# Keys of two batches turned by VectorE through DRAM instead of by TensorE

## The chip, the cores and the metric

One of the cores of a Trainium2 chip runs the kernel. The metric is the device time of one execution in microseconds: before the change the median of 3 runs is 856.25 us (856.16 to 856.46).

## The reference, cut to what matters

Linear attention over 4 batches, 8 heads, 576 positions and 64 numbers per head; its output goes through two feed-forward layers (512 to 2048 to 512), the first with ELU, the second with Mish. All in float32.

```python
q_s = softmax(q, axis=-1)                      # over the 64 numbers of a head
k_s = softmax(k, axis=2)                       # over the 576 positions
kv  = einsum('bhsd,bhse->bhde', k_s, v)        # 64 x 64 per head
x   = einsum('bhsd,bhde->bhse', q_s, kv)       # heads side by side: 2304 x 512
h   = x @ w_in;  g = where(h > 0, h, exp(min(h, 0)) - 1);  x = g @ w_out
h   = x @ w2_in; g = h * tanh(log1p(exp(min(h, 20))));     out = g @ w2_out
```

## The kernel before

**Numbers.** The weights come as 64-bit numbers, 512 KB for a piece of 128 rows. A piece is loaded raw, its exponent is moved by ScalarE (`rebias`), it is put together by VectorE (`decode`), and it is split into a high and a low part (`split_piece`: ScalarE the high one, GpSimd the low one). Activations are split the same way, and each product is three matmuls: low times high, high times low, high times high.

**Blocks and slots.** The 18 tiles of 128 tokens form five blocks of 4, 3, 4, 3 and 4 tiles (`TILES`), so 512 or 384 columns. Layer 1 goes block by block; a block has 16 slots, one for each piece of 128 hidden numbers. In slot f TensorE makes h of piece f (12 matmuls, `mm_h`), then whatever else the slot holds, and then adds piece f-2 to the output y (12 matmuls, `mm_y`). y has four PSUM banks, and the last slot of a block is followed by `end_y`, which splits them into the input of layer 2; that is emitted at the end of slot 1 of the next block, and each bank is free for the new block when ScalarE has copied its high part and VectorE has subtracted it. Two DMAs on GpSimd's queue then store the two parts to DRAM, 1 MB each for block 0. Layer 2 starts after block 4.

**What lies beside it.** While block j runs, the attention of the next tiles is made, and raw pieces of layer 2's weights are loaded, split and stored to DRAM. The function `at(j, f, where, ...)` puts a step into a slot, and `where` is its place there: "pre", "load", "mid", "pe", "post", "last", "late", in this order for every engine's queue; nothing is reordered later. The steps of head pair hp of a batch (two heads, 128 rows of the transposed key, 576 positions in five chunks of 128, the last with 64) count from slot s = 2 hp - 1 in blocks 1 and 2 (where batches 2 and 3 are made):

- `load_k` in s-2 and `load_v` in s+2, both by SyncE. There are three key buffers (`kT`) and one value buffer (`v`).
- `k_max` (VectorE) and `k_exp` (ScalarE) in s, with the positions along the free dimension.
- `k_turn` and `k_turn_rest` in s+1: TensorE transposes four chunks of 128 and one of 64 into PSUM; `k_turned` and `k_turned_rest`: ScalarE copies them back into the same tile.
- `k_kv` in s+3: the product of the turned key with the value, 20 passes in the trace. It stands ahead of the transposes of the next head pair in the same slot.
- `k_scale`: ScalarE scales it into the block-diagonal tile that `q_x` uses.

Query tiles already go another way in blocks 1 to 3: `q_out` stores the tile to DRAM, `q_in` fetches it back by four DMAs, one for each group of 32 partitions, so that 32 x 32 blocks change places, and `q_blocks` lets VectorE transpose every 32 x 32 block in place. `q_x` then multiplies the tile with the block-diagonal tile. SyncE issues all of these DMAs in the order of the program, and an issue that waits holds all behind it.

The constants by name: `P` is 128, `DM` is 512, `NC` is 5 (chunks of positions), `NHP` is 4 (head pairs). `L263` and so on in the rows are lines of the program before: 263 `k_turn`, 280 `k_turn_rest`, 297 `k_kv`, 428 `mm_h`, 477 `mm_y`, 487 `end_y`, 241 `k_max`, 359 and 364 `q_sum` and `q_norm`, 332 `q_blocks`, 154 `decode_low`, 161 `decode_join`, 443 `elu_join`, 461 `split_lo`, 218 `load_k`, 225 and 229 `load_v`, 319 `q_out`, 326 `q_in`, 133 a raw piece.

Of the kernel before, what the change touches and what calls it, by code (L numbers as in the profile page):

```python
# [8 lines left out]
F32 = mybir.dt.float32  # L9
F32R = mybir.dt.float32r  # L10
U32 = mybir.dt.uint32
# [5 lines left out]
P = 128  # L17
# [23 lines left out]
def attention_elu_mish(  # L41
# [15 lines left out]
    nc = tc.nc  # L57
    B, DM, S = kT.shape
# [3 lines left out]
    NHP = DM // P  # L62
# [6 lines left out]
    TILES = (4, 3, 4, 3, 4)  # L69
    NA = len(TILES)  # L70
    assert sum(TILES) * P == NT
    at0 = [sum(TILES[:j]) for j in range(NA)]
# [42 lines left out]

    raw = {}
    w_hi, w_lo, split_t = {}, {}, {}
    w_src = {("i", 0): w1_in, ("o", 0): w1_out, ("i", 1): w2_in, ("o", 1): w2_out}  # L120

    def load_piece(kind, layer, f, t=None):
        w = w_src[kind, layer]
        if t is None:
            t = stage.tile([P, 512, 2], U32, tag="raw", name="raw", bufs=4)
        c = slice(f * P, (f + 1) * P)
        if kind == "i":
            nc.sync.dma_start(
                out=t.rearrange("p (k c) two -> p k (c two)", c=P),
                in_=w[:, c, :].rearrange("(k p) c two -> p k (c two)", p=P),  # L130
            )
        else:
            nc.sync.dma_start(out=t, in_=w[c, :, :])
        raw[kind, layer, f] = t
# [75 lines left out]
    def load_k(b, hp, t=None):  # L210
        if t is None:
            t = ap.tile([P, NC, P], F32, tag="kT", name="kT", bufs=3)
        en_t[b, hp] = t

        if S % P:
            nc.gpsimd.memset(t[S % P:P, S // P, S % P:P], 0.0)
        t = t.rearrange("p c e -> p (c e)")[:, 0:S]
        nc.sync.dma_start(out=t, in_=kT[b, hp * P:(hp + 1) * P, :])
        k_t[b, hp] = t
# [13 lines left out]
    def load_q(i, t=None):  # L233
        if t is None:
            t = ap.tile([P, DM], F32, tag="q", name="q")
        nc.sync.dma_start(out=t, in_=q[i * P:(i + 1) * P, :])
        q_t[i] = t
# [13 lines left out]
    def inverse(s):  # L251
        nc.vector.tensor_scalar(out=s, in0=s, scalar1=EPS, scalar2=None, op0=ALU.add)
        nc.vector.reciprocal(out=s, in_=s)
# [60 lines left out]

    R = 32

    def q_out(i):
        d = dram.tile([P, DM], F32, name=f"turn_q{i}")
        nc.sync.dma_start(out=d, in_=q_t[i])
        turn_t[i] = d  # L320

    def q_in(i):

        d = turn_t.pop(i).rearrange("(a j) (h r i) -> r j h a i", j=R, r=P // R, i=R)
        for r in range(P // R):
            nc.sync.dma_start(
                out=q_t[i][r * R:(r + 1) * R, :].rearrange("j (h a i) -> j h a i", h=NHP, i=R),
                in_=d[r],
            )

    def q_blocks(i):
        nc.vector.transpose(out=q_t[i], in_=q_t[i])

    NH = DM // D

# [1 line left out]
        return q_t[i].rearrange("p (h d) -> p h d", d=D)  # L337

    def load_q3(i):
        t = ap.tile([P, NC, P], F32, tag="kT", name="kT", bufs=3)  # L340
        load_q(i, t.rearrange("p c e -> p (c e)")[:, 0:DM])

    def q_max(i):
        m = sp.tile([P, NH], F32, tag="qm", name="qm")
# [272 lines left out]
    def at(j, f, where, fn, *a):  # L617
        j, f = j + f // NF, f % NF
        beside.setdefault((j, f, where), []).append((fn, a))
# [5 lines left out]
    def kv_chain(j, f, b):  # L625
        for hp in range(NHP):

            s = f + 2 * hp
            if j or hp > 2:
                at(j, s - 2, "load", load_k, b, hp)  # L630
            if (b, hp) not in v_t:
                at(j, s + 2, "load", load_v, b, hp)
            at(j, s, "late", k_max, b, hp)
            at(j, s, "late", k_exp, b, hp)
            at(j, s + 2, "post", lambda b, hp: inverse(rk_t[b, hp]), b, hp)
            at(j, s + 3, "post", k_scale, b, hp)


            rest = s + 1 if j else s + 2
            if j and hp:  # L640
                at(j, s + 1, "pe", k_kv, b, hp - 1)
            at(j, rest, "pe", k_turn_rest, b, hp)
            at(j, rest, "pe", k_turned_rest, b, hp)
            if not j or hp == NHP - 1:
                at(j, s + 3, "pe", k_kv, b, hp)
            at(j, s + 1, "pe", k_turn, b, hp)
            at(j, s + 1, "pe", k_turned, b, hp)

    def q_chain(j, f, i, o):
        at(j, f - 2, "late", load_q3 if j and o == 2 else load_q, i)  # L650
        at(j, f - 1, "late", q_max, i)
        at(j, f - 1, "late", q_less, i, NORM[j])
        at(j, f, "mid", q_exp, i)
        at(j, f, "late", q_sum, i)
        at(j, f, "late", q_norm, i, NORM[j])
        for fn in (q_x, x_hi, x_lo):
            at(j, f + (5 if j else 2), "pe", fn, i)
        if j:
            at(j, f + 1, "late", q_out, i)
            at(j, f + 2, "late", q_in, i)  # L660
            at(j, f + 4, "post", q_blocks, i)
            return
        for fn in (q_turn, q_turned):
            at(j, f + 1, "pe", fn, i)
# [11 lines left out]
    for j in range(NA - 1):  # L676
        if j + 1 < B:
            kv_chain(j, -1 if j else 0, j + 1)
        for o in range(TILES[j + 1]):
            q_chain(j, 9 - 3 * (TILES[j + 1] - 1 - o) if j else 8 + 2 * o, at0[j + 1] + o, o)  # L680

    for n in range(NF):
        j, s = 1 + n // 4, n % 4 * 4
# [241 lines left out]
```

## Time and profile before

| what | us |
|---|---|
| median of 3 runs | 856.25 |
| the profiled execution | 856.38 |
| its span, first to last instruction | 854.6 |
| TensorE busy | 843.7 (99% of the span) |
| VectorE busy | 599.4 (70%) |
| ScalarE busy | 451.1 (53%) |
| GpSimd busy | 160.3 (19%) |

The granted clock of TensorE is 0.999 of full speed over the span. An engine's busy time counts its own instructions, not the issue of DMAs; a matmul's duration overlaps with the next, so what a matmul costs is read from the distance between two starts. Block 1 runs from about 121.9 to 199.9 us and block 2 from there to about 286 us.

### The profile page before, as it was taken

How to read it: one execution, taken by the hardware profiler on the slowest of the kernel's cores; microseconds unless marked ns; L12 is line 12 of the kernel's file. 1: busy time of each engine (PE TensorE's matmuls, PEld its weight loads, DVE VectorE, ACT ScalarE, POOL GpSimd, SP SyncE). 2: the span in 40 equal slices, each digit the busy share in tenths (PEclk: the TensorE clock that was granted, in tenths of full speed). 3: DMA queues.
4: the chain of work that ended last, by engine and by line, in shares of the span. 5: the costliest groups of instructions: out<-in, count | busy, mean ns of one | idle time of the engine just before them, and what ended most of it. 6: DMA issues, size and time to landing. Idle time of an engine off the chain costs nothing.

```text
span 854.6 us, 11819 instructions
## 1 busy us (share of the span) xinstructions
PE 843.7 (99%) x4364; PEld 728.6 (85%) x4364; DVE 599.4 (70%) x1051; ACT 451.1 (53%) x854; POOL 160.3 (19%) x210
## 2 busy tenths in 40 slices
PE   7999999999999999999999999999999999999998
PEld 5778889998888899988889998888888888888996
DVE  7899866665555577554446877777787777777776
ACT  7797757656554465554444444444444444444443
POOL 4366523233212242223332000000000000000000
PEclk9999999999999999999999999999999999999999
DMA  9791648673845196538876003000210021000101
GB/s 302 251 306 55 197 129 279 182 231 98 232 131 161 52 265 196 166 99 286 278 243 227 1 0 103 34 1 0 99 50 1 0 74 50 1 1 1 50 1 37
DMA packets 79865, 104.05 MB, mean 122 GB/s; under 512 B 27328, under 2 KB 56256, under 8 KB 77248
## 3 DMA queue, kind: packets, MB, share of 16 engines
q1 hardware_dynamic: 63536, 58.08, 22.8%
q0 software_dynamic: 16128, 45.09, 16.0%
q8 instruction: 34, 0.56, 0.3%
q14 instruction: 23, 0.19, 0.1%
q10 hardware_dynamic: 144, 0.13, 0.0%
HBM read 73.14 MB, written 30.15 MB: 121 GB/s over the span
## 4 chain that ended last, share of the span: by engine, by line
PE 95%; ACT 1%; issue 1%; POOL 1%; DVE 1%; DMA 0%; SPq 0%; POOLq 0%; ACTq 0%
PE h L428 45%; PE y L477 23%; PE y L565 15%; PE a L565 8%; PE a L388 2%; PE a L297 1%; PE a L263 1%; DMA q<-in_q_dram 0%; POOL wil L186 0%; PE a L280 0%; DVE qs L359 0%; ACT early L148 0%; PE a L374 0%; ACT woh L180 0%; POOL wol L186 0%
## 5 line engine op out<-in xcount | busy, mean ns | idle before, releaser
L443 DVE SCALAR_TENSOR_TENSOR e<-h,e 128x512 f32<-128x512 f32 (+1 forms) x80 | 50.9, 636 | 106.7 <-ACT e L439 106.2
L428 PE MATMUL h<-xha,wih 128*128 128x512 f32 (+1 forms) x328 | 125.0, 385 | 0.7 <-ACT xha L404 0.7
L428 PE MATMUL h<-xla,wih 128*128 128x512 f32 (+1 forms) x328 | 125.2, 385 | 0.4 <-DVE xla L408 0.4
L428 PE MATMUL h<-xha,wil 128*128 128x512 f32 (+1 forms) x328 | 125.2, 385 | 0.3 <-POOL wil L186 0.3
L533 ACT ACTIVATE r<-n,two 128x512 f32<-128x512 f32 (+1 forms) x80 | 54.6, 682 | 131.1 <-DVE n L529 131.1
L477 PE MATMUL y<-gh,wol 128*128 128x512 f32 (+1 forms) x320 | 120.1, 377 | 0.3 <-POOL wol L186 0.3
L477 PE MATMUL y<-gh,woh 128*128 128x512 f32 (+1 forms) x320 | 117.4, 368 | 0.0
L477 PE MATMUL y<-gl,woh 128*128 128x512 f32 (+1 forms) x320 | 117.2, 368 | 0.0
L435 ACT ACTIVATE e<-h 128x512 f32<-128x512 f32 (+1 forms) x80 | 44.5, 556 | 115.9 <-PE h L428 115.8
L428 PE MATMUL h<-xhb,wih 128*128 128x384 f32 (+1 forms) x304 | 104.7, 344 | 0.0
L428 PE MATMUL h<-xhb,wil 128*128 128x384 f32 (+1 forms) x304 | 104.6, 344 | 0.0
L428 PE MATMUL h<-xlb,wih 128*128 128x384 f32 (+1 forms) x304 | 104.4, 344 | 0.0
L186 POOL TENSOR_TENSOR lo<-raw,hi 128x512 fp32r<-128x512 f32 x32 | 43.9, 1372 | 229.9 <-ACT hi L180 144.8
L512 ACT ACTIVATE u<-h 128x512 f32<-128x512 f32 (+1 forms) x80 | 44.1, 551 | 72.1 <-PE h L428 72.1
L522 DVE TENSOR_SCALAR u<-u 128x512 f32<-128x512 f32 (+1 forms) x80 | 32.0, 400 | 64.9 <-ACT u L512 63.6
L565 PE MATMUL y<-woh,gl 128*128 128x512 f32 x192 | 75.2, 392 | 0.0
L565 PE MATMUL y<-woh,gh 128*128 128x512 f32 x192 | 75.1, 391 | 0.0
L565 PE MATMUL y<-wol,gh 128*128 128x512 f32 x192 | 74.7, 389 | 0.0
L461 DVE TENSOR_TENSOR gl<-e,gh 128x512 fp32r<-128x512 f32 (+1 forms) x80 | 52.4, 656 | 28.6 <-ACT gh L457 28.5
L428 PEld LDWEIGHTS h<-xha,wih 128*128 128x128 f32 x328 | 61.1, 188 | 13.2 <-ACT xha L404 0.9
L428 PEld LDWEIGHTS h<-xha,wil 128*128 128x128 f32 x328 | 61.1, 188 | 12.9 <-POOL wil L186 0.9
L457 ACT ACTIVATE gh<-e 128x512 fp32r<-128x512 f32 (+1 forms) x80 | 47.0, 588 | 47.3 <-PE y L477 39.3
(163 smaller groups left out, 1755.8 us busy)
## 6 DMA issues: line engine op xcount, KB each, us to landing
raw<-in_moe_w_out_dram SPq DMA_DIRECT2D x23, 512.0 KB, 4.9
raw<-in_moe_w_in_dram SPq DMA_DIRECT2D x21, 512.0 KB, 5.2
early<-in_moe_w_in_dram SPq DMA_DIRECT2D x11, 512.0 KB, 6.3
early<-in_moe_w_out_dram SPq DMA_DIRECT2D x9, 512.0 KB, 6.5
out_dram<-o SPq DMA_DIRECT2D x17, 256.0 KB, 2.0
w2ih<-hi POOLq DMA_DIRECT2D x16, 256.0 KB, 2.7
w2il<-lo POOLq DMA_DIRECT2D x16, 256.0 KB, 3.8
w2oh<-hi POOLq DMA_DIRECT2D x16, 256.0 KB, 3.3
```

The lines of the kernel that those rows point to most:

```text
L186: nc.gpsimd.tensor_tensor(out=lo, in0=z, in1=hi.bitcast(F32), op=ALU.subtract)
L388: nc.tensor.matmul(out=ps[:, hp, t0:t1], lhsT=kvbd[b % 2][:, hp, :], rhs=u[:, hp, t0:t1], start=True, stop=True,)
L428: nc.tensor.matmul(out=h_t[f][:, c], lhsT=w[:, i, k * P:(k + 1) * P], rhs=x[k][:, c], start=(n == 0), stop=(n == 3 * KD - 1),)
L435: nc.scalar.activation(out=e, in_=h_t[f], func=AF.Exp)
L443: nc.vector.scalar_tensor_tensor(out=e, in0=h_t[f], scalar=0.0, in1=e, op0=ALU.max, op1=ALU.subtract)
L457: nc.scalar.activation(out=gh_t[f], in_=h_t[f], func=AF.Copy)
L461: nc.vector.tensor_tensor(out=gl_t[f], in0=h_t.pop(f), in1=gh_t[f].bitcast(F32), op=ALU.subtract)
L477: nc.tensor.matmul(out=y_t[e][:, 0:gh.shape[1]], lhsT=w[:, i, e * P:(e + 1) * P], rhs=x, start=(f == 0 and n == 0), stop=(f == NF - 1 and ...
L512: nc.scalar.activation(out=u, in_=h_t[f], func=AF.Exp)
L522: nc.vector.tensor_scalar(out=u, in0=u, scalar1=U_MAX, scalar2=None, op0=ALU.min)
L533: nc.scalar.activation(out=r, in_=n, func=AF.Ln, bias=two)
L565: nc.tensor.matmul(out=y_t[p, t], lhsT=x[:, c], rhs=w[:, i, :], start=(f == 0 and n == 0), stop=(f == NF - 1 and n == 2),)
```

## The change

Batches 2 and 3 no longer have their keys turned on TensorE. After `k_exp` the whole tile of 640 columns goes to DRAM (`k_out`, slot s+1), comes back by four DMAs with its 32 x 32 blocks exchanged (`k_in`, slot s+2), and VectorE transposes the blocks in place (`k_blocks`, slot s+3). The product and its scaling move from s+3 to s+4, the loads of values from s+2 to s+3, and the loads of keys go to the end of their slot. The zeroed part of the tile's last chunk grows from 64 to 128 partitions.

Query tiles in blocks 1 to 3 start one slot later, and `q_x` stays in its slot. One query tile in three used to borrow a key buffer; it now has a buffer of its own, the fourth of the raw pieces, which layer 2's pieces give up.

```diff
         if t is None:
-            t = stage.tile([P, 512, 2], U32, tag="raw", name="raw", bufs=4)
+            n = len(raw_use) % (4 if layer == 0 else 3)
+            raw_use.append(n)
+            t = stage.tile([P, 512, 2], U32, tag=f"raw{n}", name="raw", bufs=1)
...
-            nc.gpsimd.memset(t[S % P:P, S // P, S % P:P], 0.0)
+            a = 0 if b > 1 else S % P
+            nc.gpsimd.memset(t[a:P, S // P, S % P:P], 0.0)
...
+    def turn_out(key, t, n):
+        d = dram.tile([P, n * P], F32, name="turn_" + "_".join(map(str, key)))
+        nc.sync.dma_start(out=d, in_=t)
+        turn_t[key] = d
+
+    def turn_in(key, t, n):
+
+        d = turn_t.pop(key).rearrange("(a j) (c r i) -> r j c a i", j=R, r=P // R, i=R)
         for r in range(P // R):
             nc.sync.dma_start(
...
+                out=t[r * R:(r + 1) * R, :].rearrange("j (c a i) -> j c a i", c=n, i=R), in_=d[r]
+            )
+
+    def turn_blocks(t):
+        nc.vector.transpose(out=t, in_=t)
+
+    def k_all(b, hp):
+        return en_t[b, hp].rearrange("p c e -> p (c e)")
+
+    def k_out(b, hp):
+        turn_out(("k", b, hp), k_all(b, hp), NC)
+
+    def k_in(b, hp):
+        turn_in(("k", b, hp), k_all(b, hp), NC)
+
+    def k_blocks(b, hp):
+        turn_blocks(k_all(b, hp))
...
     def load_q3(i):
-        t = ap.tile([P, NC, P], F32, tag="kT", name="kT", bufs=3)
-        load_q(i, t.rearrange("p c e -> p (c e)")[:, 0:DM])
+        load_q(i, stage.tile([P, 4 * 512 // 2], F32, tag="raw3", name="q3", bufs=1)[:, 0:DM])
...
             if j or hp > 2:
-                at(j, s - 2, "load", load_k, b, hp)
+                at(j, s - 2, "late" if j else "load", load_k, b, hp)
             if (b, hp) not in v_t:
-                at(j, s + 2, "load", load_v, b, hp)
+                at(j, s + 3, "load", load_v, b, hp)
...
+            if j:
+                at(j, s + 1, "late", k_out, b, hp)
+                at(j, s + 2, "late", k_in, b, hp)
+                at(j, s + 3, "post", k_blocks, b, hp)
+                at(j, s + 4, "pe", k_kv, b, hp)
+                at(j, s + 4, "post", k_scale, b, hp)
+                continue
             at(j, s + 3, "post", k_scale, b, hp)
...
-        at(j, f - 2, "late", load_q3 if j and o == 2 else load_q, i)
+        at(j, f - 2, "late", load_q3 if j and i % 3 == 0 else load_q, i)
...
-            at(j, f + (5 if j else 2), "pe", fn, i)
+            at(j, f + (4 if j else 2), "pe", fn, i)
...
-            at(j, f + 4, "post", q_blocks, i)
+            at(j, f + 3, "post", q_blocks, i)
...
-            q_chain(j, 9 - 3 * (TILES[j + 1] - 1 - o) if j else 8 + 2 * o, at0[j + 1] + o, o)
+            q_chain(j, 10 - (3 if j else 2) * (TILES[j + 1] - 1 - o) if j else 8 + 2 * o, at0[j + 1] + o, o)
```

**TensorE, slot 2 of block 1, before.** `h` and `y` are the outputs of `mm_h` and `mm_y`, `a` a bank of the attention.

```order
L428 MATMUL h<-xlb,wih 128x384
L428 MATMUL h<-xhb,wih 128x384
L297 MATMUL a<-v,kT 64x64 x10
L280 MATMUL a<-ident,kT 64x128
L263 MATMUL a<-ident,kT 128x128 x4
L477 MATMUL y_1512<-gh,wol 128x384
```

Now the same slot on TensorE, where `mm_y` has become line 499 and `mm_h` line 450:

```order
L450 MATMUL h<-xhb,wil 128x384
L450 MATMUL h<-xlb,wih 128x384
L450 MATMUL h<-xhb,wih 128x384
L499 MATMUL y_1484<-gh,wol 128x384
L499 MATMUL y_1484<-gl,woh 128x384
```

Nothing stands between h and y there any more; the product of the first head pair is in slot 3, alone.

**VectorE, slots 1 and 2 of block 1, before.** `ks` and `km` are the sum and the maximum of a key, `xla` the low part of block 0's y, whose four banks are y_509 to y_512.

```order
L461 TENSOR_TENSOR gl<-e,gh 128x384
L443 SCALAR_TENSOR_TENSOR e<-h,e 128x384
L252 TENSOR_SCALAR ks<-ks 128x1
L253 RECIPROCAL ks<-ks 128x1
L241 TENSOR_REDUCE km<-kT 128x1
L487 TENSOR_TENSOR xla<-y_509,xha 128x512
L487 TENSOR_TENSOR xla<-y_510,xha 128x512
```

Now the same place on VectorE:

```order
L244 TENSOR_REDUCE km<-kT 128x1
L381 TENSOR_REDUCE qs<-q 128x8
L255 TENSOR_SCALAR qs<-qs 128x8
L256 RECIPROCAL qs<-qs 128x8
L386 TENSOR_TENSOR q<-q,qs 128x512
L509 TENSOR_TENSOR xla<-y_509,xha 128x512
L509 TENSOR_TENSOR xla<-y_510,xha 128x512
L509 TENSOR_TENSOR xla<-y_511,xha 128x512
L509 TENSOR_TENSOR xla<-y_512,xha 128x512
L156 TENSOR_SCALAR raw<-raw 128x512
L163 SCALAR_TENSOR_TENSOR raw<-raw 128x512
L483 TENSOR_TENSOR gl<-e,gh 128x384
```

The four steps of query tile 7 stood one slot earlier; they are now ahead of the reading of y's banks.

**SyncE, slots 1 to 4 of block 1, before.** `q_1278` is query tile 7, `kT_1549` the key of head pair 3, `v_1545` the value of head pair 1.

```order
L236 DMA q_1435<-in_q_dram 128x512
L128 DMA raw_1478<-in_moe2_w_in_dram 128x4x256
L326 DMA q_1278<-turn_q7_1433 32x16x32 x4
L225 DMA v_1545<-in_v_dram 128x4x128
L229 DMA v_1545<-in_v_dram 64x128
L218 DMA kT_1549<-in_kT_dram 128x576
L133 DMA raw_1606<-in_moe2_w_out_dram 128x1024
```

Now the same place on SyncE, where `q_1323` is query tile 7, `kT_1320` and `kT_1551` the keys of head pairs 1 and 3, and `v_1592` the value of head pair 1:

```order
L322 DMA turn_k_2_1_1478<-kT_1320 128x640
L322 DMA turn_q_7_1480<-q_1323 128x512
L239 DMA q_1482<-in_q_dram 128x512
L329 DMA kT_1320<-turn_k_2_1_1478 32x20x32 x4
L221 DMA kT_1551<-in_kT_dram 128x576
L329 DMA q_1323<-turn_q_7_1480 32x16x32 x4
L228 DMA v_1592<-in_v_dram 128x4x128
L232 DMA v_1592<-in_v_dram 64x128
L135 DMA raw_1596<-in_moe2_w_out_dram 128x1024
L322 DMA turn_k_2_2_1605<-kT_1418 128x640
```

The value of head pair 1 stands behind eight transfers of the two exchanges and the key load of head pair 3.

## Rows read from the trace of the kernel before

**Rows 1.** The page, busy time, share of the span and instructions of an engine.

```profile
PE 843.7 (99%) x4364; PEld 728.6 (85%) x4364; DVE 599.4 (70%) x1051; ACT 451.1 (53%) x854; POOL 160.3 (19%) x210
```

**Rows 2.** The page, the chain that ended last, by engine.

```profile
PE 95%; ACT 1%; issue 1%; POOL 1%; DVE 1%; DMA 0%; SPq 0%; POOLq 0%; ACTq 0%
```

**Rows 3.** Busy us of PE, PEld, DVE, ACT, POOL; clock, DMA share, GB/s.

```profile
121.90:199.90 78.00, 78.00 (x519) 75.12 (x517) 50.99 (x96) 47.01 (x100) 21.39 (x34) 1.00 0.69 209
199.90:286.00 86.10, 86.10 (x478) 72.05 (x477) 46.38 (x82) 46.65 (x90) 18.69 (x27) 1.00 0.53 149
```

**Rows 4.** Timeline of TensorE, slot 6 of block 1: start us, us, instruction.

```profile
152.09 0.33 PE L428 MATMUL h<-xlb,wih 128*128 128x384 f32 x1
152.26 0.34 PE L428 MATMUL h<-xhb,wih 128*128 128x384 f32 x1
152.53 0.80 PE L297 MATMUL a<-v,kT 128*64 128x64 f32 x20
153.26 0.30 PE L280 MATMUL a<-ident,kT 128*64 128x128 f32 x1
...
153.76 0.42 PE L477 MATMUL y<-gh,wol 128*128 128x384 f32 x1
```

**Rows 5.** Timeline of TensorE, slot 0 of block 1.

```profile
121.57 0.34 PE L428 MATMUL h<-xhb,wih 128*128 128x384 f32 x1
...
122.21 0.47 PE L477 MATMUL y<-gh,wol 128*128 128x512 f32 x1
```

**Rows 6.** Timeline of TensorE, slot 2 of block 1.

```profile
131.86 0.34 PE L428 MATMUL h<-xhb,wih 128*128 128x384 f32 x1
...
133.35 0.42 PE L477 MATMUL y<-gh,wol 128*128 128x384 f32 x1
```

**Rows 7.** Timeline of VectorE, slots 0 to 2 of block 1.

```profile
123.55 0.69 DVE L359 TENSOR_REDUCE qs<-q 128x8 f32<-128x512 f32 x1
...
124.72 0.69 DVE L364 TENSOR_TENSOR q<-q,qs 128x512 f32<-128x512 f32 x1
...
129.17 0.73 DVE L241 TENSOR_REDUCE km<-kT 128x1 f32<-128x576 f32 x1
131.33 2.48 DVE L487 TENSOR_TENSOR xla<-y,xha 128x512 fp32r<-128x512 f32 x4 [1.42 <-ACT xha L486]
133.73 0.42 DVE L154 TENSOR_SCALAR raw<-raw 128x512 uint32<-128x512 uint32 x1
...
134.79 0.55 DVE L461 TENSOR_TENSOR gl<-e,gh 128x384 fp32r<-128x384 f32 x1
```

**Rows 8.** Groups by line: busy us, mean ns, idle us before.

```profile
L154 DVE TENSOR_SCALAR raw<-raw 128x512 uint32<-128x512 uint32 x44 | 27.8, 640 | 0.0
...
L332 DVE STREAM_TRANSPOSE q<-q 128x512 f32<-128x512 f32 x8 | 5.6, 703 | 0.1
```

**Rows 9.** Timeline of SyncE's queue, slots 3 to 6 of block 1.

```profile
133.00 0.39 SPq L225 DMA_DIRECT2D v<-in_v_dram  x1
133.43 0.52 SPq L229 DMA_DIRECT2D v<-in_v_dram  x1
134.05 1.36 SPq L218 DMA_DIRECT2D kT<-in_kT_dram  x1
135.46 1.16 SPq L133 DMA_DIRECT2D raw<-in_moe_w_out_dram  x1
142.45 0.33 SPq L319 DMA_DIRECT2D turn_q<-q  x1
...
147.02 2.66 SPq L326 DMA_DIRECT2D q<-turn_q  x4
```

**Rows 10.** DMAs issued from 132.9 to 135.6 us: KB each, us to landing.

```profile
x2l<-xla POOLq DMA_DIRECT2D x1, 1024.0 KB, 7.9
...
kT<-in_kT_dram SPq DMA_DIRECT2D x1, 288.0 KB, 8.2
...
v<-in_v_dram SPq DMA_DIRECT2D x1, 32.0 KB, 5.4
```

More of the change, by code (lines that the diff above doesn't have):

```diff
@@ L114, in attention_elu_mish @@
     stage = att.enter_context(tc.tile_pool(name="stage", bufs=2))
-    raw = {}
+    raw, raw_use = {}, []
     w_hi, w_lo, split_t = {}, {}, {}
@@ L315, in attention_elu_mish, with q_out, q_in @@
     R = 32
[L317 to L324, printed above, removed]
+    def turn_out(key, t, n):
[4 more added lines that the diff above has]
+        d = turn_t.pop(key).rearrange("(a j) (c r i) -> r j c a i", j=R, r=P // R, i=R)
         for r in range(P // R):
             nc.sync.dma_start(
-                out=q_t[i][r * R:(r + 1) * R, :].rearrange("j (h a i) -> j h a i", h=NHP, i=R),
-                in_=d[r],
-            )
+                out=t[r * R:(r + 1) * R, :].rearrange("j (c a i) -> j c a i", c=n, i=R), in_=d[r]
+            )
+    def turn_blocks(t):
[8 more added lines that the diff above has]
+        turn_blocks(k_all(b, hp))
+    def q_out(i):
+        turn_out(("q", i), q_t[i], NHP)
+    def q_in(i):
+        turn_in(("q", i), q_t[i], NHP)
     def q_blocks(i):
-        nc.vector.transpose(out=q_t[i], in_=q_t[i])
+        turn_blocks(q_t[i])
     NH = DM // D
@@ L635, in kv_chain @@
             at(j, s + 2, "post", lambda b, hp: inverse(rk_t[b, hp]), b, hp)
-            at(j, s + 3, "post", k_scale, b, hp)
[L639 to L645, printed above, removed]
+            if j:
[5 more added lines that the diff above has]
+                continue
+            at(j, s + 3, "post", k_scale, b, hp)
+            at(j, s + 2, "pe", k_turn_rest, b, hp)
+            at(j, s + 2, "pe", k_turned_rest, b, hp)
+            at(j, s + 3, "pe", k_kv, b, hp)
             at(j, s + 1, "pe", k_turn, b, hp)
```

## The prediction

> **What bounds the kernel now.** First the busy times: TensorE works 843.7 us, 99% of the span [rows 1]. Then the chain that ended last: 95% of it is TensorE's own work [rows 2]. The change touches blocks 1 and 2 only, so next the table by stage: in 121.9 to 199.9 us (block 1) and 199.9 to 286.0 us (block 2) TensorE is busy every microsecond, VectorE 65% and 54%, and the DMA engines are busy 69% and 53% of the time [rows 3]. So a microsecond taken from TensorE in these two stretches comes off the whole, if nothing new makes it wait; a microsecond taken from ScalarE does not. Then the order of time on TensorE, to see what the edited pieces cost between two ordinary matmuls, and last the queues of VectorE and SyncE beside them.
>
> **What is removed from TensorE.** Eight head pairs (four each of batches 2 and 3) lose one short and four full transposes. In six of eight places they follow the key-value product in the same slot: the short transpose starts at 153.26 and the first y matmul at 153.76 [rows 4], so 0.50 us each, 3.0 us. In the other two (the first head pair of a batch) they stand alone: from the last h matmul to the first y matmul 122.21 - 121.57 = 0.64 us [rows 5], where two matmuls of this width follow each other after 152.26 - 152.09 = 0.17 us [rows 4]: 0.47 us each, 0.94 us. Sum 3.94 us. No row shows a y matmul directly behind a key-value product; entering the product costs 0.27 - 0.17 = 0.10 us more than a plain step [rows 4], so leaving it costs between nothing and 0.1 us in eight places, 0 to 0.8 us. I take nothing, since the short transpose follows it without a gap (20 passes in 0.73 us).
>
> **What is given back in block 1, in three places, each a wait that the removed work covered.** All times below are those of the trace less what TensorE has saved by then.
>
> 1. The banks of y. Slot 0 saves 0.47 us. In slot 2 the product moves away too (to slot 3), so 133.35 - 131.86 - 0.17 = 1.32 us of cover go [rows 6]: TensorE stands before the first y of block 1 at 133.35 - 0.47 - 1.32 = 131.56. These banks hold block 0's y until VectorE has subtracted the high part. Tile 7's sum, inverse and scaling now stand in slot 1, ahead of that, 124.72 + 0.69 - 123.55 = 1.86 us of VectorE; the key maximum before them ends at 129.17 + 0.73 = 129.90, or 129.43 after the saving; so the four subtractions, 2.48 us together, run from 131.29 and free a bank at 131.91, 132.53, 133.15 and 133.77 [rows 7]. A bank takes TensorE 3 x 0.17 = 0.52 us, so it ends at 134.29 instead of 131.56 + 2.08 = 133.64: 0.65 us lost.
> 2. The first product. VectorE goes on with a piece's decode (134.79 - 133.73 = 1.06 us), a split and an elu of about 0.55 us each [rows 7], then the new block transpose: 128x512 takes 0.70 us [rows 8], so 128x640 about 0.88 (0.70 if it were a fixed cost, 1.05 if it grew faster). It ends at 133.77 + 1.06 + 1.10 + 0.88 = 136.8. TensorE, after 12 matmuls of h, is there at 134.29 + 2.08 = 136.37: 0.43 us lost.
> 3. The value tile of head pair 1. It has one buffer, so its load is behind the first product; what matters is what stands ahead of it in SyncE's queue. Before: nothing but that wait. Now: four transfers of keys (issued by then), the load of head pair 3's keys, which waits for the first product's key buffer, and tile 7's four transfers. The product ends at 136.8 + 0.73 = 137.5. The load's issue takes 0.66 us, as each of tile 7's four (2.66 for four), or 1.36 us as the one at 134.05; then 2.66 us [rows 9]. The value load goes out at 140.85 (141.55). Its second, 32 KB part goes out 0.43 us later, and in this stretch it landed 5.4 us after its issue [rows 9, 10]: 146.7 (147.4). TensorE wants it after another four groups of 12: 137.6 + 4 x 2.08 = 145.95. Late by 0.7 us (1.4); I take 0.7, the nearer to the many quick issues. From below the bound is 0, from above the slowest landing of that stretch, 8.2 us for keys while the two 1 MB stores of block 0's result were under way [rows 10]: 140.85 + 8.2 - 145.95 = 3.1 us.
>
> In block 2 the order is the same, but a pair of slots, four groups of 12 matmuls, lasts 4 x 2.08 / 3 = 2.8 us longer (512 columns instead of 384) while SyncE's and VectorE's work is the same, and tile 11 comes three slots later than tile 7 does: nothing is late there.
>
> **What costs nothing, and why.** VectorE gains 8 x 0.88 = 7.0 us in stretches where it idles 27 and 40 us [rows 3]; ScalarE loses its eight pairs of copies out of PSUM, off the path. Tile loads and transfers of queries move by one slot, but their products stay in the same slots. Three raw buffers instead of four: a piece's buffer must be free about five slots before its decode, and it was given up two slots earlier still; none of the 44 decodes of raw pieces ever had VectorE idle before it [rows 8]. If that cover went, ScalarE's and VectorE's queues would stop at the piece, with VectorE's third of block 1 idle to catch up in.
>
> **The sum.** -3.94 + 0.65 + 0.43 + 0.7 = -2.16 us. The profiled execution took 856.38 us, so 854.2; the runs shown have a median of 856.25, 0.13 lower: 854.1 us.
>
> One rule speaks against this. The new transfers into SBUF move runs of 32 numbers, 128 bytes. Tile 7's kind of transfer, the same runs, shows a queue that takes four of them in 2.66 us and no wait behind it on TensorE [rows 9]. The Trainium skill, "DMA: Bandwidth & Descriptors", section Specifications, puts the smallest transfer at line rate at 512 bytes and gives 435 GB/s as the ceiling; if 128 bytes went at a quarter of that, an estimate from the page is 320 KB in 3.0 us instead of 0.75. By it the key and query transfers ahead of the value load would hold it up to 4 us longer, and the sum would be up to +1.9 us, 858.1. What it would do here is the second case below (the late value tile), which is worked out without the page.
>
> **Rivals.**
> - No new wait bites: the subtractions or the value load come in time. For it: SyncE stands idle from 136.6 to 142.4 us [rows 9]. Against: VectorE's row of work in slot 1 leaves no room. -3.94 us, 852.3.
> - The value tile lands as late as the slowest load of that stretch, 3.1 us: -3.94 + 0.65 + 0.43 + 3.1 = +0.24, 856.5. For it: the stores of 1 MB are in the same stretch, and keys issued there took 8.2 us [rows 10]. Against: the value load goes out when most of the stores have landed.
> - Slower: SyncE's queue becomes the bound of block 1. A pair of slots asks of it: key store and the wait for its landing 4.57 us (as 142.45 to 147.02), four key transfers about 3.0, a query tile's four 2.66, keys 1.36, values 1.05, a piece 1.16 [rows 9]: 13.8 us, where TensorE needs 4 x 2.08 + 0.83 = 9.2 us. Some 2 us of it fit into the wait for the key store. If no more does, the second product is late by 3.1 us and the third and fourth by 2 to 3 us each: +0.24 + 4 to 6, 860.5 to 862.5. It decides if the third head pair's first transfer is issued later than about 149 us. For it: nearly every issue waits for something in the same slot. Against: a query tile comes only with every third slot, not with every second.
>
> **How the numbers follow.** My forecast 0.50, its own range 852.8 to 855.2 (leaving the product 0.1 us dearer in eight places, the value load between on time and 1.4 us late); no wait 0.10; the late value tile 0.20; SyncE as bound 0.20. A measurement of this kernel tells 0.2% (1.7 us) from no change. Of the forecast 0.43 lies below 854.5; with the 0.10, faster 0.53. Slower (over 858.0) 0.21, all of the last case and a little of a late tile with a second one behind it. Same 0.26. Range 852.2 to 858.5: it leaves out most of the last case and little below.
>
> **What would show it.** Right: key-value products followed at once by y in blocks 1 and 2; TensorE idle about 0.6 us before the first y of block 1 (released by VectorE's subtraction), 0.4 us before the first product of batch 2 (released by the block transpose), and under 1.5 us before the second (a load); none of it in block 2. Wrong: TensorE waiting on the third and fourth product, VectorE idle before a block transpose for more than 2 us, or waits in block 2; or no waits at all.

## The result, and the profile after

The change makes the kernel slower. Its median is 860.69 us (860.31 to 863.23) against 856.24 for the kernel before; the ratio is 1.0057, 95% interval 1.0042 to 1.0072. The profiled execution took 860.48 us with a span of 858.7 us, both 4.1 us more than before. The prediction, 854.1 with a range up to 858.5, was wrong in sign.

These lines of the page answer to [rows 1, 2]: busy time of each engine, and the chain that ended last, by engine.

```profile
PE 843.8 (98%) x4324; PEld 726.5 (85%) x4324; DVE 604.4 (70%) x1059; ACT 446.4 (52%) x838; POOL 160.7 (19%) x210
PE 90%; DMA 5%; DVE 2%; ACT 1%; SPq 1%; issue 1%; POOL 0%; POOLq 0%; DVEq 0%; ACTq 0%
```

Forty instructions have left TensorE, yet it is busy as long as before: some of its work has become slower. In the chain DMA now has 5% where it had 0%. The table by stage answers to [rows 3]:

```profile
121.90:199.90 78.00, 73.80 (x473) 70.33 (x472) 50.13 (x96) 41.17 (x85) 19.38 (x30) 0.98 0.84 227
199.90:286.00 86.10, 86.10 (x461) 71.43 (x460) 50.78 (x89) 46.09 (x87) 21.87 (x33) 1.00 0.70 190
```

In block 1 TensorE now stands idle for 4.2 us, its mean clock is 0.98, and the DMA share has risen from 0.69 to 0.84. Block 2 is full as before. Next the timeline of TensorE at slot 5 of block 1 (start, duration, instruction; in brackets the idle time before it and what ended it):

```profile
145.40 0.34 PE L450 MATMUL h<-xhb,wih 128*128 128x384 f32 x1
148.51 0.69 PE L300 MATMUL a<-v,kT 128*64 128x64 f32 x16 [2.77 <-DMA v<-in_v_dram]
149.73 0.34 PE L300 MATMUL a<-v,kT 128*64 128x64 f32 x4 [0.53 <-DMA v<-in_v_dram]
150.07 1.89 PE L410 MATMUL a<-q,kvbd 128*128 128x128 f32 x8
151.62 0.67 PE L499 MATMUL y<-gh,wol 128*128 128x384 f32 x1
...
154.74 0.33 PE L450 MATMUL h<-xhb,wil 128*128 128x384 f32 x1
```

The second product waits for the value tile, first for its large part, then for its 32 KB part. Without a wait the query product would start at 145.40 + 0.27 + 0.73 = 146.40; it starts at 150.07, 3.7 us late. Behind it the work itself is slow: the query product takes 151.62 - 150.07 = 1.55 us, where an undisturbed one takes 0.81, and twelve y matmuls take 154.74 - 151.62 = 3.12 us instead of 12 x 0.173 = 2.08. The granted clock (third figure from the end) tells why:

```profile
150.00:151.00 1.00, 0.99 (x8) 0.96 (x6) 0.97 (x3) 0.00 (x0) 0.20 (x1) 0.62 1.11 404
151.00:152.00 1.00, 1.00 (x6) 1.00 (x6) 0.00 (x0) 0.00 (x0) 0.00 (x0) 0.50 1.07 339
152.00:153.00 1.00, 1.00 (x4) 1.00 (x4) 0.37 (x1) 0.99 (x3) 0.00 (x0) 0.50 0.28 82
...
154.00:155.00 1.00, 1.00 (x8) 1.00 (x7) 0.90 (x3) 0.73 (x2) 0.00 (x0) 1.00 0.53 83
```

After the idle stretch TensorE was at the 1.2 GHz level, and from 154 on at 2.4 GHz again. That costs 0.74 + 1.04 = 1.8 us. SyncE's queue of the same stretch answers to [rows 9]:

```profile
133.88 6.48 SPq L329 DMA_DIRECT2D kT<-turn_k  x4
140.47 1.03 SPq L221 DMA_DIRECT2D kT<-in_kT_dram  x1
141.54 2.67 SPq L329 DMA_DIRECT2D q<-turn_q  x4
144.31 0.95 SPq L228 DMA_DIRECT2D v<-in_v_dram  x1
```

The four key transfers took 6.48 us to issue; the first head pair's four, at 122.85, took 2.75. GpSimd issues the two 1 MB stores of block 0's result in the same stretch:

```profile
132.33 0.53 POOL L521 DMA_DIRECT2D x2h<-xha  x1 [0.80 <-ACT xha L508]
133.84 0.53 POOL L521 DMA_DIRECT2D x2l<-xla  x1 [0.98 <-DVE xla L509]
```

So the long issue stands right beside them. The value load goes out at 144.31, 3.5 us after the forecast of 140.85. TensorE's first y of block 1, and VectorE's steps that the prediction priced, answer to [rows 6, 7]:

```profile
131.81 0.44 PE L499 MATMUL y<-gh,wol 128*128 128x384 f32 x1 [0.34 <-DVE xla L509]
...
131.07 2.48 DVE L509 TENSOR_TENSOR xla<-y,xha 128x512 fp32r<-128x512 f32 x4
...
135.46 0.83 DVE L334 STREAM_TRANSPOSE kT<-kT 128x640 f32<-128x640 f32 x1
...
147.59 0.71 DVE L334 STREAM_TRANSPOSE q<-q 128x512 f32<-128x512 f32 x1 [2.41 <-DMA q<-turn_q]
```

The last line shows a second late operand, hidden behind the value tile: tile 7's block transpose waited for its transfers and ended at 147.59 + 0.71 = 148.30, so the query product would have been 1.9 us later than 146.40 even with the value tile in time.

At equal points of the program the delay against before grows like this (starts of the same h matmul; slot 14's stands ahead of the block's last query product):

| place | before | after | delay | added |
|---|---|---|---|---|
| block 1, slot 0 | 119.81 | 119.64 | -0.17 | |
| block 1, slot 14 | 189.70 | 194.50 | +4.80 | +4.97 |
| block 2, slot 14 | 282.12 | 285.34 | +3.22 | -1.58 |
| block 3, slot 14 | 356.62 | 360.68 | +4.06 | +0.84 |

Block 2 gains about what it should. Block 1 loses 5 us, and block 3, where no keys are turned at all, loses 0.84.

### The profile page after: what moved, and what is told of

It reads as the page before. It is cut to its first block, busy times and chain, and to the rows that moved or that the text cites. A ratio compares the mean times of both kernels' runs of the same rounds, so it can differ in the third digit from the quotient of the medians.

```text
span 858.7 us, 11824 instructions
## 1 busy us (share of the span) xinstructions
PE 843.8 (98%) x4324; PEld 726.5 (85%) x4324; DVE 604.4 (70%) x1059; ACT 446.4 (52%) x838; POOL 160.7 (19%) x210
## 4 chain that ended last, share of the span: by engine, by line
PE 90%; DMA 5%; DVE 2%; ACT 1%; SPq 1%; issue 1%; POOL 0%; POOLq 0%; DVEq 0%; ACTq 0%
PE h L450 43%; PE y L499 21%; PE y L587 15%; PE a L587 8%; PE a L410 2%; DMA early_x<-in_v_dram 1%; DMA early<-in_moe_w_out_dram 1%; PE a L300 1%; DMA early<-in_v_dram 1%; DMA turn_k<-kT 1%; DMA kT<-turn_k 1%; SPq L329 1%; DMA early<-in_kT_dram 1%; DMA v<-in_v_dram 0%; ACT e L457 0%
## 5 line engine op out<-in xcount | busy, mean ns | idle before, releaser
L450 PEld LDWEIGHTS h<-xla,wih 128*128 128x128 f32 x328 | 61.2, 188 | 12.5 <-DVE xla L430 0.5
```

Of the source, the lines that this page charges most:

```text
L450: nc.tensor.matmul(out=h_t[f][:, c], lhsT=w[:, i, k * P:(k + 1) * P], rhs=x[k][:, c], start=(n == 0), stop=(n == 3 * KD - 1),)
```

## The experiments

All ratios are to the kernel before, with 95% intervals.

**First round: the value tile, the clock, and the parts.** The theory was that the value tile's place in the queue, and the clock behind the wait, explain block 1. Its rival: the DMA traffic holds up whatever comes.

*value2*: a second value buffer, loaded one slot earlier.

```diff
-            t = ap.tile([P, NC, P], F32, tag="v", name="v", bufs=1)
+            t = ap.tile([P, NC, P], F32, tag="v", name="v", bufs=2)
...
-                at(j, s + 3, "load", load_v, b, hp)
+                at(j, s + 2, "load", load_v, b, hp)
```

> All of the change kept; the value tile gets a second buffer (its 2,560 bytes come from giving the high parts of layer 2's pieces the unused half of the fourth raw buffer), and its load stands one slot earlier in SyncE's queue, ahead of the four key transfers of the same head pair. Theory (late value tile): the 3.3 us wait before and inside the second product of block 1 go, and with the wait the stretch at 1.2 GHz behind it (about 1.8 us): 860.7 - 3.5 - 1.8 = 855.4, granted clock 1.00 throughout. Rival (traffic): the DMA engines are full between 136 and 150 us, whoever comes first in the queue only swaps places, and TensorE waits over 2 us for the block transpose of the second head pair instead, and the clock falls all the same: 859 to 861.

861.38 us, 1.0059 (1.0046 to 1.0071). The rival won, though its wait of over 2 us came as two of 1.8 and 1.9. TensorE at slot 5:

```profile
147.96 0.80 PE L306 MATMUL a<-v,kT 128*64 128x64 f32 x20 [1.83 <-DVE kT L340]
150.66 1.62 PE L416 MATMUL a<-q,kvbd 128*128 128x128 f32 x6 [1.89 <-DVE q L340]
```

And SyncE's queue ahead of it:

```profile
132.41 1.20 SPq L234 DMA_DIRECT2D v<-in_v_dram  x1
...
134.41 7.97 SPq L335 DMA_DIRECT2D kT<-turn_k  x4
```

The value tile is in time, and now the keys are late, then the query tile: the four key transfers took 7.97 us to issue. Behind these waits the granted clock was at 0.50 again from 151 to 154 us. The wait only changed its name, so the value tile's place in the queue was not the cause.

*filled_wait*: sixteen matmuls that nobody reads, in the wait.

```diff
+        if (b, hp) == (2, 1):
+            for n in range(16):
+                nc.tensor.matmul(
+                    out=ps[:, P:], lhsT=w_hi["i", 0, 1][:, 1, 0:P], rhs=xh[1][:, 0, :],
```

> All of the change kept; 16 matmuls of 128x384 whose result nobody reads stand on TensorE ahead of the second product of block 1, where it waits for the value tile (16 x 0.17 = 2.8 us of the wait of 2.9). Theory (the low clock follows from the idle time): the granted clock stays at 1.00 behind the wait, the product for tile 7 takes 0.81 us instead of 1.55 and the 24 matmuls behind it 4.2 instead of 5.2: 860.7 - 1.8 = 858.9. Rival (those matmuls were slow for another reason, such as the transfers under way): still 0.5 to 0.67 of the clock and 860.7, or more if the 16 matmuls come too late.

860.07 us, 1.0051 (1.0039 to 1.0064). Its TensorE:

```profile
145.59 2.94 PE L299 MATMUL a<-xhb,wih 128*128 128x384 f32 x16
149.07 1.01 PE L306 MATMUL a<-v,kT 128*64 128x64 f32 x20 [0.55 <-DVE q L340]
150.09 1.13 PE L416 MATMUL a<-q,kvbd 128*128 128x128 f32 x8
150.97 0.42 PE L505 MATMUL y<-gh,wol 128*128 128x384 f32 x1
...
160.29 0.80 PE L306 MATMUL a<-v,kT 128*64 128x64 f32 x20 [0.74 <-DMA raw<-in_moe_w_in_dram]
```

The microsecond of its table that was the slowest in the change:

```profile
151.00:152.00 1.00, 1.00 (x8) 1.00 (x8) 0.64 (x3) 0.74 (x2) 0.00 (x0) 1.00 1.22 395
```

The clock stays at 1.00 with the DMA engines as full as in the change, and the query product takes 0.88 us: the slow matmuls came from the low clock that followed the idle time. But of the 1.8 us only about 0.6 reach the end: 0.6 between the medians, with runs that overlap, and 0.7 between the profiled executions (slot 14 of block 1 at 193.82 instead of 194.50). The third product comes earlier now and waits 0.74 us. Its keys were turned by 157.81; its value tile, issued at 155.69 and 156.12, took about 4 us to land, which TensorE's lateness had covered in the change. (The row names a raw piece that was issued behind it in the same queue.)

*batch3_only* and *tiles_late_only* keep parts of the change: the keys of batch 3 alone, or no keys. The others get the steps of the kernel before, written out where the diff has "...".

```diff
             s = f + 2 * hp
+            if j == 1:     # batch3_only; in tiles_late_only always
+                ...
+                continue
```

> Batch 2 (block 1) turned by TensorE as before, batch 3 (block 2) by VectorE; query tiles and raw buffers as in the change. Theory (the change pays in block 2, its loss is in block 1): block 2 gains the 1.6 us that it gained in the change, block 1 neither gains nor loses, and block 3 loses 0.8 us for the query tiles that come one slot later (see the next run): 856.2 - 1.6 + 0.8 = 855.4. Rival (the transfers of keys cost TensorE as much as the transposes did, in either block): 856.2 to 857.5.

> Keys of batches 2 and 3 turned by TensorE as before; kept of the change are the query tiles that load, normalize and go to DRAM one slot later, their third buffer and three raw buffers. Theory (banks): in block 3 the sum and scaling of a query tile now stand ahead of VectorE's four subtractions out of the banks, and the first y of the block waits: 0.8 us there and 0 to 0.4 in block 1, 857.0 to 857.4. Rival (tiles and raw buffers are free): 856.2.

batch3_only: 855.89 us, 0.9996 (0.9987 to 1.0005); at the points of the table block 2 gains 1.58 us and block 3 loses 0.86. tiles_late_only: 858.41 us, 1.0028 (1.0018 to 1.0038), more than forecast. It has no new transfer, and yet TensorE stands twice in block 3:

```profile
303.82 0.34 PE L450 MATMUL h<-xhb,wih 128*128 128x384 f32 x1
304.50 0.44 PE L499 MATMUL y<-gh,wol 128*128 128x384 f32 x1 [0.33 <-DVE xla L509]
...
318.88 1.13 PE L410 MATMUL a<-q,kvbd 128*128 128x128 f32 x8 [1.40 <-DVE q L334]
```

Its SyncE issues tile 14's transfers while block 2's stores (2 MB) run:

```profile
308.09 4.89 SPq L329 DMA_DIRECT2D q<-turn_q  x4
```

So the one slot that the query tiles lose has two prices: VectorE's sum and scaling come ahead of the four subtractions that free the banks, and the tile's transfers move into the stores. In the kernel before they were issued ahead of them, at 300.18, in 2.61 us. The change itself paid only the first: in its block 3 TensorE waits at the banks and nowhere else.

**Second round: the stores.** New theory: while the 1 MB stores run, SyncE cannot issue the exchange's transfers at its usual pace.

*stores_away*, and later its control *before_stores_away*, the same edit on the kernel before:

```diff
+        if not j and not early:
+            return
         for b, o, t, n in runs:
...
+    at(0, 8, "late", end_y, 0, True)
```

> All of the change kept; the two 1 MB stores of block 0's result no longer stand at the start of block 1 but in slot 8 of block 0, where they store the block's x instead of its y (so the output is another). Theory (the stores hold up the four key transfers of the second head pair: 6.5 us of issue instead of 2.7, and with them all that is behind them in SyncE's queue): the four are issued in under 3.5 us, value tile and query tile are there in time, no wait at the second product and no low clock: 860.7 - 3.5 - 1.8 = 855.4. Rival (the runs of 128 bytes themselves are slow): still 6 us of issue, still a wait of 2 to 3 us, 860 to 861.

> The kernel before, with the two 1 MB stores of block 0's result in slot 8 of block 0 (holding x instead of y, so the output is another). It is the control for stores_away. Theory (TensorE waits for nothing in the kernel before): no difference, 856.5. Rival (the stores cost TensorE something by themselves, or save it something where they stood): another time by 1 us or more, and stores_away has to be read against that.

The control: 856.41 us, 0.9999 (0.9991 to 1.0008), so the stores cost the kernel before nothing. stores_away: 856.94 us, 1.0004 (0.9995 to 1.0013). Its SyncE:

```profile
134.68 2.64 SPq L329 DMA_DIRECT2D kT<-turn_k  x4
...
138.05 2.59 SPq L329 DMA_DIRECT2D q<-turn_q  x4
140.74 0.62 SPq L228 DMA_DIRECT2D v<-in_v_dram  x1
```

And its TensorE at slot 5:

```profile
145.54 0.34 PE L450 MATMUL h<-xhb,wih 128*128 128x384 f32 x1
145.81 0.80 PE L300 MATMUL a<-v,kT 128*64 128x64 f32 x20
146.54 1.16 PE L410 MATMUL a<-q,kvbd 128*128 128x128 f32 x8
```

The same instructions in the same order, without the stores: 2.64 us, the value load at 140.74 (forecast for the change: 140.85), no wait at the second product, clock 1.00; slot 14 of block 1 is reached at 190.60 instead of 194.50. So the stores beside the four transfers are the cause of the long issue and of what was late behind it. The time is 1.5 us above what was expected; 1.2 of it are waits that now stand at the third and fourth product, 0.62 and 0.56 us.

*tiles_early, keys_early, keys_late*: the query tiles back in their old slots; the keys of batch 2 as in the change, one slot earlier (with the second value buffer), one slot later.

```diff
-            q_chain(j, 10 - (3 if j else 2) * (TILES[j + 1] - 1 - o) if j else 8 + 2 * o, at0[j + 1] + o, o)
+            q_chain(j, 9 - 3 * (TILES[j + 1] - 1 - o) if j else 8 + 2 * o, at0[j + 1] + o, o)
...
-            kv_chain(j, -1 if j else 0, j + 1)
+            kv_chain(j, (0, -2, -1)[j], j + 1)   # keys_early; keys_late: (0, 0, -1)
```

> Of the change everything but the schedule of the query tiles, which are loaded, normalized and sent to DRAM one slot earlier again, as before (block transpose and product in the same slots as in the change). Theory: the sums no longer stand ahead of the four subtractions (block 3 gets its 0.8 us back, block 1 some 0.4), and tile 7's four transfers are issued before the two 1 MB stores, so that the value load is 2.7 us earlier: it is late by under 1 us, and no low clock follows: 860.7 - 1.2 - 2.7 - 1.8 = 855.0. Rival (only the banks matter; the key transfers wait for the stores whatever stands beside them): 860.7 - 1.2 = 859.5.

> As the run before, and the keys of batch 2 two things more: their chain stands one slot earlier, so that the second head pair's four transfers are issued ahead of the two 1 MB stores, and the value tile has its second buffer with the load a slot earlier. Theory: no wait in block 1 and none at the start of block 3; what is left is the removed transposes (-3.9, of which handing over from product to y took some 0.35 back): 856.2 - 3.6 = 852.7. Rival (VectorE, 80% busy at the end of block 0, or SyncE's queue in front of the third head pair, is late instead): 854.5 to 857.

> Query tiles as in the run tiles_early, one value buffer; the keys of batch 2 one slot later, so that the second head pair's transfers are issued when most of the two 1 MB stores have landed. Theory: they take about 2.7 us to issue, the second product comes two slots behind the first with its value tile in time: 852.7 to 853.5. Rival (the stores only shift the wait to the query tile 7 or to the first head pair): over 855.

861.59 us, 1.0061 (1.0049 to 1.0074); 857.33, 1.0012 (1.0003 to 1.0021); 860.52, 1.0048 (1.0035 to 1.0061). All three theories miss; of the rivals that of keys_late holds, and that of keys_early misses by 0.3 us. The longest line of SyncE's queue tells why, in tiles_early,

```profile
136.36 7.10 SPq L329 DMA_DIRECT2D kT<-turn_k  x4
```

in keys_early,

```profile
136.24 6.57 SPq L335 DMA_DIRECT2D q<-turn_q  x4
```

and in keys_late:

```profile
131.54 5.58 SPq L329 DMA_DIRECT2D q<-turn_q  x4
```

Whoever stands there pays, and what is behind is late: the value tile again in tiles_early (2.9 us of waiting) and in keys_late (5.1 us). tiles_early waits at the third and fourth product as well, 1.1 and 2.1 us. In all three, block 3 has its 0.84 us back.

**Third round: short runs, or the stores alone?** *plain_rows* and *plain_all* bring whole rows back.

```diff
         for r in range(P // R):
-            nc.sync.dma_start(
-                out=t[r * R:(r + 1) * R, :].rearrange("j (c a i) -> j c a i", c=n, i=R), in_=d[r]
-            )
+            nc.sync.dma_start(out=t[r * R:(r + 1) * R, :], in_=d[r * R:(r + 1) * R, :])
```

> All of the change kept, but the four key transfers out of DRAM bring each row back as one run of 2,560 bytes, instead of 20 runs of 128 bytes (nothing is exchanged, so the products are other numbers). Theory (SyncE's issue is held because the 1 MB stores fill the DMA engines, whatever the length of the runs): the second head pair's four still take 5 us or more, the value tile is late and the clock falls: 859 to 861. Rival (the 128-byte runs are what is slow beside the stores): under 3 us of issue, the value load goes out 3.5 us earlier, no wait over 0.5 us at the second product: 855.4 to 856.

> All of the change kept, but the transfers of keys and of queries out of DRAM bring each row back as one run of 2,560 or 2,048 bytes instead of runs of 128 bytes (nothing is exchanged, so the output is another). Theory (SyncE is held where many short runs stand beside the 1 MB stores; either alone is harmless): no four transfers take over 3 us to issue, the value load goes out before 141 us and no wait over 0.5 us at the second product; the banks still cost 0.4 and 0.8 us: 855 to 856. Rival (the stores hold everything that is issued beside them): as plain_rows, 858.3, or more.

858.33 us, 1.0020 (1.0012 to 1.0029), and 856.45 us, 0.9998 (0.9989 to 1.0007). SyncE in plain_rows:

```profile
132.43 2.24 SPq L345 DMA_DIRECT2D kT<-turn_k  x4
...
137.64 5.01 SPq L329 DMA_DIRECT2D q<-turn_q  x4
...
156.00 3.45 SPq L329 DMA_DIRECT2D q<-turn_q  x4
```

SyncE in plain_all:

```profile
133.08 2.25 SPq L329 DMA_DIRECT2D kT<-turn_k  x4
...
138.28 3.63 SPq L329 DMA_DIRECT2D q<-turn_q  x4
...
155.38 1.79 SPq L329 DMA_DIRECT2D q<-turn_q  x4
```

Neither time forecast for plain_rows came true: its keys were quick, as the rival said, but the queries behind them, still in runs of 128 bytes, took 5.01 us, and the value tile was late by 1.8 us. plain_all came out 0.5 us above its range.

With whole rows the keys take 2.25 us beside the stores (1.97 at 123.64, ahead of them). One reserve stays on them: in both runs their issue began 1.4 and 0.8 us earlier than in the change, right behind the first store and 1.4 us ahead of the second. Two pairs of rows are closer to each other. At nearly the same time beside the stores, the queries took 5.01 us in short runs and 3.63 in whole rows. And tile 8's queries, in both runs behind a 512 KB piece and a key store of SyncE's own queue, took 3.45 and 1.79. So short runs hold SyncE longer where other transfers run, and not beside the stores alone. But whole rows are held beside the stores too: 3.63 us is over the 3 that was expected of plain_all, and its value tile is late by two waits of 0.26 and 0.39 us.

The Trainium skill, "Perfetto Trace Analysis", section "What 'DMA-bound' means", says that a solid stretch on the issuing engine is the making of descriptors, not the moving of data, and that large descriptors help. That large ones help, these rows bear out (1.79 us instead of 3.45); that the same four transfers took 2.64 us in stores_away and 6.48 in the change is no matter of their descriptors alone. What SyncE waited for, and which resource was full, no run here shows.

**Fourth round: a version that avoids it.** *batch3_tiles* is batch3_only with the query tiles in their old slots (first line of the diff above).

> Batch 2 turned by TensorE as before, batch 3 by VectorE as in the change, query tiles on the slots of before. Theory (the change pays where no 1 MB store stands beside its transfers; the tiles' later slot cost block 3 its 0.8 us): block 2 gains the 1.6 us of the run batch3_only and block 3 loses nothing: 856.3 - 1.6 = 854.7. Rival (tile 14's transfers stand one slot earlier and other waits take the place of the bank): 855.9 as in batch3_only, or no less than before.

855.41 us, 0.9987 (0.9978 to 0.9995), faster than before, though 0.7 us short of the forecast. *keys_apart* turns all eight pairs and places batch 2's around the stores; *keys_apart_2* also loads a value tile earlier, *keys_apart_3* the query tiles too (last line).

```diff
+            kv = s + 4
+            load = s + 3
+            if j == 1:
+                s, kv = ((-3, 1), (-1, 3), (2, 7), (4, 9))[hp]
+                load = (0, 2, 4, 8)[hp]              # keys_apart: kv - 1
...
-        at(j, f - 2, "late", load_q3 if j and i % 3 == 0 else load_q, i)
+        at(j, f - 2, "load" if j else "late", load_q3 if j and i % 3 == 0 else load_q, i)
```

> All eight head pairs turned by VectorE, query tiles on the slots of before, and the four of batch 2 so placed that none of their transfers out of DRAM is issued in the 10 us of the 1 MB stores: the first two head pairs two slots earlier (products in slots 1 and 3), the last two with one slot more between exchange and product (slots 7 and 9). Theory (the stores hold whatever SyncE issues beside them for 4 us or more, and nothing else is wrong with the change): no wait over 0.5 us, clock 1.00, 856.3 - 3.9 + 0.35 = 852.7. Rival (VectorE at the end of block 0, 80% busy, or tile 7's query transfers in the stores make TensorE wait): 854 to 857.

> As keys_apart, but the third head pair's value load stands two slots earlier in SyncE's queue, ahead of the transfers of its keys and of query tile 8, since its buffer is free from slot 3 on. Theory (the runs of keys_apart lay between 853.8 and 860.3 because that load sometimes misses its product, by 3.0 us in the profiled run, and a low clock follows): every run near the quickest of keys_apart, 853.0 to 854.5. Rival (SyncE's queue is late by the 8.8 us that tile 7's four transfers took in the stores, whoever stands where): again spread over 854 to 860.

> As keys_apart_2, but the query tiles of blocks 1 to 3 are loaded at the start of their slot, ahead of the key transfers of the same slot in SyncE's queue. Theory (in keys_apart_2 TensorE's 2.4 us in front of the third product came from VectorE, which had waited 2.9 us for tile 9's load, queued behind the third head pair's four transfers): that wait goes, clock 1.00, runs near 853. Rival (block 1 has no room for both exchanges beside the stores, a wait turns up elsewhere): again 854 to 859, spread.

keys_apart: 857.84 us, 1.0007 (0.9992 to 1.0022), its executions between 853.8 and 860.3. keys_apart_2: 856.32, 0.9999 (0.9987 to 1.0012), between 853.1 and 859.3, not what the theory expected but the spread of its rival. In both, tile 7's four transfers took over 8.5 us beside the stores. But TensorE's 2.4 us in front of the third product had a nearer cause, in VectorE's line of keys_apart_2:

```profile
153.75 0.69 DVE L367 TENSOR_REDUCE qm<-q 128x8 f32<-128x512 f32 x1 [2.90 <-DMA q<-in_q_dram]
...
157.22 0.84 DVE L334 STREAM_TRANSPOSE kT<-kT 128x640 f32<-128x640 f32 x1
```

A query load, queued behind key transfers, held the block transpose that stands behind that maximum. keys_apart_3, with the query tiles loaded earlier: 853.23 us (852.56 to 854.63), 0.9964 (0.9950 to 0.9977), faster than both kernels. Its SyncE:

```profile
129.62 3.00 SPq L329 DMA_DIRECT2D q<-turn_q  x4
...
142.42 2.80 SPq L329 DMA_DIRECT2D kT<-turn_k  x4
```

Its table by stage:

```profile
121.90:199.90 78.00, 78.00 (x509) 75.17 (x509) 54.45 (x98) 44.88 (x93) 21.44 (x32) 1.00 0.81 227
199.90:286.00 86.10, 86.10 (x462) 70.97 (x460) 49.26 (x86) 43.60 (x82) 19.48 (x29) 1.00 0.70 191
```

No exchange out of DRAM is issued between 132.6 and 142.4, and TensorE is busy all the time in both blocks. The earlier loads did two things at once: the wait of VectorE is gone, and tile 7's four transfers went out ahead of the stores, in 3.00 us instead of the 8.59 of keys_apart_2. Which of the two mattered more this run does not tell, and its five executions are few beside the spread of keys_apart_2's twelve.

## Why the prediction was wrong

- **What is removed, 3.94 us: right, 0.4 too much.** In keys_apart_3, where nothing waits, slot 14 of block 3 is reached at 352.78 instead of 356.62; less the 0.26 us by which that run was ahead at the start of block 1 already, that is 3.6. The rest, under 0.05 us in each of eight places, lies inside the bound named for leaving the product (0 to 0.1).
- **Step 1, the banks, 0.65 us: right; 0.84 measured.** From the last h of slot 2 (131.14) to that of slot 3 (136.14) it is 5.00 us where 24 x 0.173 = 4.16 would do. VectorE's subtractions began at 131.07 (forecast 131.29).
- **Step 2, the first product, 0.43 us: did not happen.** TensorE was there when forecast (136.41 instead of 136.37), but VectorE was 0.5 us ahead: the block transpose ended at 136.29, forecast 136.8. Its subtractions began 0.2 us earlier, and the sum had added durations that overlap: from the split's start to the block transpose's it took 135.46 - 134.53 = 0.93 us instead of 1.10.
- **Step 3, the value tile, 0.7 us: the step that failed.** The place was right, the size was not: 3.7 us, above the upper bound of 3.1. The wrong part is "four transfers of keys (issued by then)". They took 6.48 us to issue, beside the 1 MB stores; with the stores moved away (stores_away) they took 2.64, and the value load went out at 140.74. [Rows 9] showed four such transfers in 2.66 us, but at 147, when the stores had landed. The bound from [rows 10] held a late landing beside the stores, and not that SyncE itself would be held there, with everything behind it. The same long issue made tile 7's query late as well, by 1.9 us, hidden behind the value tile; the prediction had put the query transfers at nothing because their products stayed in their slots. value2 shows that wait (1.89 us).
- **The clock: not priced.** The wait brought 1.8 us of low clock with it; by filled_wait some 0.6 of it counted at the end.
- **"The change touches blocks 1 and 2 only": wrong.** The query tiles move in block 3 too, and there the new order of VectorE ahead of the banks cost 0.84 us. From slot 14 of block 2 to that of block 3 batch3_tiles needs 74.49 us, batch3_only 75.36.
- **Block 2, nothing late: right** (-1.58 of 1.8 possible). Four key transfers took 4.33 us there beside two stores, and its longer slots covered it.
- **The sum with the measured sizes.** In block 1: 0.84 + 3.7 + 1.8, two small waits (0.3 in front of the fourth product, 0.6 at tile 9's), less 1.97 for four pairs, make 5.3; the table has 4.97, and the rest stays open.
- **The rivals.** The slower one gave 860.5 to 862.5 and the time lies there, but by another route. It had SyncE's queue too short by a sum over every pair of slots, with the third and fourth product 2 to 3 us late each. They were late by 0 and 0.3, though its mark was passed (the third pair's first transfer went out at 151.65, after 149): TensorE was late itself. With the stores gone (stores_away) these two products wait 0.6 us each, in tiles_early, with the stores, 1.1 and 2.1. The second rival, the late value tile, had the mechanism and 3.1 us for it; it lacked the clock and block 3.
- **The rule on short transfers** (the Trainium skill, "DMA: Bandwidth & Descriptors", section Specifications, line rate from 512 bytes on) had been set aside by a row from a quiet stretch. That row holds for a quiet stretch: without the stores four transfers in short runs took 2.64 us. Beside other transfers the length of the runs mattered (5.01 us against 3.63, 3.45 against 1.79). The value load went out 3.5 us late, inside the 4 us that the prediction worked out by the rule, but moving the stores brought nearly all of that back with the runs as short as before.
- **Its own range, 852.8 to 855.2, does not follow from the two terms named for it.** Those, 0 to 0.8 us for leaving the product and 0.7 us either way for the value load, give 853.4 to 855.6, so the chance of 0.43 that was read off below 854.5 was too high.

## What to carry to other kernels

Before a transfer is added to a queue, look at what the other queues move in that stretch: its issue time read where the DMA engines are free (2.7 us) said nothing about a stretch with large stores (3.5 to 9 us), and what stands behind it pays. A wait on TensorE is priced with the clock behind it. When a late operand is moved up and the time stays the same, change what runs beside the queue, not the order in it.

## What the runs showed of the hardware that was not expected

- Four transfers of 64 or 80 KB in runs of 128 bytes held SyncE for 2.6 to 2.8 us with little beside them, for up to 4.0 right behind a 512 KB piece of its own queue (3.98 at 152.92 in keys_apart_3), and for 3.5 to 8.8 beside the stores of a block's result from GpSimd's queue. In whole rows it was 1.7 to 2.0 us, behind a piece too, and 2.2 to 3.6 beside the stores.
- After the idle stretch of slot 5 the granted clock went from 1.00 to 0.50 and was back within 4 us; y matmuls of 384 columns went from 0.17 to 0.32 us each.
- A block transpose of 128x640 took 0.83 to 0.85 us, against 0.70 for 128x512.
